# Transposed attention blocks kept in DRAM by the row that reads them, half of q and v loaded once, and a new time table

## The chip, the cores and the metric

The kernel runs on one core of one Trainium2 chip. The metric is the time of one execution on the device, in microseconds (us). Smaller is better.

A core has a matrix engine (TensorE, PE in the profile, with its weight loads as PEld), a vector engine (VectorE, DVE), a scalar engine (ScalarE, ACT), a general engine (GpSimd, POOL) and a synchronisation engine (SyncE, SP). Each works through its own list of instructions in the order in which the program wrote them, and waits on semaphores for what the others make. All of this kernel's DMAs are issued by SP. SP does not wait for a DMA to land, unless the next instruction in its list needs what the DMA brings, or needs a buffer that something still reads.

## The reference

Attention within chunks of 64 positions, with the softmax inside the chunk; then the heads are laid side by side and go through a layer that takes the largest of three products, and an output projection. All is float32.

```python
scores = scale * np.matmul(q_c, k_c.transpose(0, 1, 2, 4, 3))     # 8 x 8 heads x 9 chunks, 64 x 64
scores = scores - np.max(scores, axis=-1, keepdims=True)
attn = np.exp(scores)
attn = attn / (np.sum(attn, axis=-1, keepdims=True) + 1e-09)
x = np.matmul(attn, v_c)                                          # -> (4608, 512)
h = np.maximum(np.maximum(x @ w1, x @ w2), x @ w3)                # 512 -> 768
out = h @ w_out                                                   # 768 -> 512
```

## The kernel before, in words

**Tiles and groups.** The 4608 rows are 36 tiles of 128 rows, and four tiles make a group; there are nine groups. For one group TensorE makes 18 blocks of "hidden" products (6 columns blocks times three weights) and four output tiles. Each float32 matrix is held as two parts, a rounded high part and the rest, and a product is three matmuls (`three`, lines 168 to 171): 128x512 each. In the planner's account a triple of them is one step of 0.6815 us. The last two groups are taken together by another scheme (`pair`), in which TensorE alone sets the pace.

**The attention of a tile.** The first 8 tiles take a plain path at the start. The other 28 are made by `attention` (from line 270). For one of them the steps are, with the names that the time table uses:

- `r0`, `r1`: q and k are loaded into the two halves of the tile `r` (line 320), `rv`: v is loaded into `rv` (line 325). In DRAM each is kept twice, so that partitions 0 to 63 and 64 to 127 receive the same numbers.
- `qh`/`ql`, `vh`/`vl` (`stack`, lines 307 and 311): ACT rounds the tile into `qs` or `vs`, and then partitions 64 to 127 are overwritten with what the rounding left over, by DVE for q and by POOL for v. The high part thus stands in the upper 64 partitions and the low part in the lower 64, and one matmul over 128 partitions adds both.
- `kh`/`kl` (lines 333 and 337): high and low part of k, in two halves `c`, side by side in `kk`.
- `s0`, `s1` with `sa0`, `sa1` (`products`, lines 289, 295, 300): four matmuls each, whose two partial results ACT and DVE bring together in `e`.
- `mx`, `sub`, `exp`, `sum`, `nrm`: the softmax, on DVE, POOL, ACT, DVE, POOL.
- `T`, `ah`, `al` (lines 379, 384, 388): DVE transposes 32x32 blocks, and ACT and DVE make the high and the low part, in one tile `ah`.
- `there` (line 393): `ah` is written to DRAM. `aa` (line 400): it is read back, once to partitions 0 to 63 and once to 64 to 127, because each row of the matmul needs pieces from four groups of 32 partitions. That is two DMAs of 512 KB. The tile `aa` has one buffer.
- `x0`, `x1` with `xa0`, `xa1` (line 289, 295, 300): the products with v, four matmuls each, and `xh`, `xl`: high and low part of the result, which the hidden products of a later group read. For the last two groups the result goes to `stage` instead.

**What sets the order.** A planner written in the kernel walks along TensorE's own work, the triples of the groups, with a clock `now`. Every step of a tile has a time in a table, relative to that tile's `s0`, and is written into the program when `now` reaches it. So the table fixes the order on each engine; when a step really runs follows from that order and from the semaphores. The first four of the 28 tiles take the table `AT`, and one of them follows another after 18 us; the other 24 take `MOVED`, with 14.9 us from one to the next. So the work of three tiles is under way at a time: TensorE meets `s0` and `s1` of tile t+1 before `x0` of tile t, and `s1` of tile t+2 behind it.

**Other steps named below.** `spill` writes the sum of two weight parts to DRAM (line 508, `whole<-f`), `output` stores finished tiles (line 480, `out_x<-ao`); both go through SP. `OPERANDS`, `FIRST_MIXED`, `SP0` and `SP1` are due times of the preparation of the last two groups.

Of the kernel before, what the change touches and what calls it, by code (L numbers as in the profile page):

```python
# [20 lines left out]
P = 128  # L21
# [11 lines left out]
MOVED = {'r0': -18.9, 'r1': -14.6, 'rv': 7.3, 'qh': -8.4, 'ql': -7.2, 'kh0': -7.1, 'kl0': -6.2, 'kh1': -5.6, 'kl1': -1.4, 'sa0': 1.3, 's1': 3.3, 'sa1': 4.3, 'mx': 4.6, 'sub': 5.9, 'exp': 6.9, 'sum': 7.9, 'nrm': 9.1, 'T': 10.5, 'ah': 11.6, 'al': 11.7, 'there': 13.9, 'aa': 16.3, 'vh': 16.8, 'vl': 18.3, 'x0': 24.6, 'xa0': 25.6, 'x1': 28.3, 'xa1': 29.6, 'xh': 30.6, 'xl': 31.4}  # L33
EVERY = [18.3, 15.6]
OPERANDS = 5.4
FIRST_MIXED = 5.6
SECOND_MIXED = 5.6
SP0 = 10.4
SP1 = 12.0
TURN = [*range(12), 20, 21, *range(12, 16), 22, 23, *range(16, 20), *range(24, 28)]  # L40
ORDER = (1, 2, 5, 6, 7, 4, 3)
C0 = 17.3
C1 = 14.9
LEAD = 1.0
# [27 lines left out]
def chunk_attn_maxout_kernel(  # L72
# [196 lines left out]
    def attention(t, x_of, col, every, stage=None, moved=()):  # L269
# [32 lines left out]
        def stack(at, low_at, name, tag, src, eng):  # L302

            @due(at)
            def _():
                st[name] = att.tile([P, 2, 4, P], F32R, name=name, tag=tag, bufs=1)
                nc.scalar.copy(out=st[name], in_=src())  # L307

            @due(low_at)
            def _():  # L310
                eng.tensor_tensor(out=st[name][64:], in0=src()[64:], in1=st[name][64:].bitcast(F32), op=ALU.subtract)  # L311


        for half, at in enumerate((at_["r0"], at_["r1"])):
            @due(at)
            def _(half=half):
                if "r" not in loaded:
                    loaded["r"] = att.tile([P, 2, 2, 4, P], F32, name="r", tag="raw", bufs=1)
                st["r"] = loaded["r"]
                nc.sync.dma_start(out=st["r"][:, half], in_=qk2[t - PLAIN][:, half])  # L320

        @due(at_["rv"])
        def _():
            st["rv"] = att.tile([P, 2, 4, P], F32, name="rv", tag="rv", bufs=1)
            nc.sync.dma_start(out=st["rv"], in_=v2[t - PLAIN])
# [64 lines left out]
        @due(at_["there"])  # L390
        def _():
            st["there"] = dram.tile([4, 64, 512], F32, name="there")
            nc.sync.dma_start(out=st["there"].rearrange("n (l k) f -> (n l) k f", k=2),
                              in_=st["ah"].bitcast(F32).rearrange("p k a n x -> p k (a n x)"))

        @due(at_["aa"])
        def _():
            st["aa"] = att.tile([P, 4, 2, 8, 32], F32R, name="aa", tag="aa", bufs=1)
            for rows in halves_of:
                nc.sync.dma_start(out=st["aa"][rows].bitcast(F32).rearrange("p n a g x -> p n (a g x)"),  # L400
                                  in_=st["there"].rearrange("n p f -> p n f"))
# [520 lines left out]
```

## Time and profile before

| what | value |
|---|---|
| time, median of 3 runs | 716.36 us (711.51, 716.36, 722.11) |
| the profiled execution | 720.41 us on the device, span of its instructions 718.6 us |
| TensorE busy | 691.3 us, 96% of the span |
| VectorE, ScalarE, GpSimd busy | 516.7, 376.5, 249.9 us |
| DMA packets of the kernel's own queue | 125.32 MB, 57.8% of 16 engines' time |

The profile shows one execution. "Busy" of an engine counts its instructions, not its waits. A group of instructions is shown as its line, engine and operation, the tile that it writes and those that it reads, its count, its busy time and the mean of one, and the idle time of the engine just before it with what ended that. The chain of waits follows the work that ended last back from its end, at each step to what released it. A DMA is shown by its issue on SP ("SPq") and by the time from its issue to its landing. The granted clock of TensorE stands in the rows by stretch (PEclk; 1.00 is full speed).

### The profile page before, as it was taken

The page shows a single profiled execution, that of the slowest core. Times are in us where ns is not written, and L with a number is a line of the kernel's source. Part 1 is how long each engine was busy: PE and PEld are TensorE (multiplying, and loading weights), DVE is VectorE, ACT ScalarE, POOL GpSimd, SP SyncE. Part 2 cuts the span into 40 slices and gives each one's busy share as a digit, 9 for nine tenths or more (in the row PEclk, how much of TensorE's full clock was granted, in tenths as well). Part 3 has the DMA queues.
Part 4 walks back from the last instruction along what each step waited for, and adds up shares of the span by engine and source line. Part 5 has one row for each costly group of instructions (what it writes and reads, how often), then busy time and mean ns, then how long its engine had stood idle before and what let it go on. Part 6 is the DMA issues. An engine that isn't in the chain of part 4 may idle for free.

```text
span 718.6 us, 9620 instructions
## 1 busy us (share of the span) xinstructions
PE 691.3 (96%) x3336; PEld 574.5 (80%) x3336; DVE 516.7 (72%) x868; ACT 376.5 (52%) x695; POOL 249.9 (35%) x182
## 2 busy tenths in 40 slices
PE   8999999998899999999999998999989999999997
PEld 5998888887778777878877777878778888888876
DVE  6699984777668876898577876788657486768630
ACT  4476754554655566566656654566555352334221
POOL 1232201333334344222432332223323438666510
PEclk9599999999999999999999999999999999999999
DMA  8765554565787879667887767677784401011011
GB/s 344 304 226 180 205 176 138 173 207 172 224 258 215 220 209 277 177 202 213 236 232 194 214 175 236 195 212 193 194 257 123 131 30 59 29 31 26 5 55 63
DMA packets 44944, 125.93 MB, mean 175 GB/s; under 512 B 4192, under 2 KB 4192, under 8 KB 44896
## 3 DMA queue, kind: packets, MB, share of 16 engines
q1 hardware_dynamic: 44896, 125.32, 57.8%
q8 instruction: 26, 0.43, 0.3%
q14 instruction: 22, 0.18, 0.1%
HBM read 98.83 MB, written 26.48 MB: 174 GB/s over the span
## 4 chain that ended last, share of the span: by engine, by line
PE 29%; DMA 15%; DVE 13%; POOL 8%; ACT 4%; issue 3%; SPq 1%; POOLq 0%; ACTq 0%; DVEq 0%
DMA aa<-there 11%; PE pm L169 8%; PE pm L171 8%; PE pm L170 8%; DMA there<-ah 4%; PE x L289 3%; POOL c L537 2%; PE s L289 2%; POOL e L667 2%; DVE c L543 2%; POOL m L670 1%; DVE e L300 1%; POOL e L186 1%; POOL f L523 1%; ACT e L295 1%
## 5 line engine op out<-in xcount | busy, mean ns | idle before, releaser
L169 PE MATMUL pm<-xh,wl 128*128 128x512 f32 (+1 forms) x516 | 201.7, 391 | 0.0
L171 PE MATMUL pm<-xh,wh 128*128 128x512 f32 (+1 forms) x516 | 200.5, 389 | 0.0
L170 PE MATMUL pm<-xl,wh 128*128 128x512 f32 (+1 forms) x516 | 200.2, 388 | 0.0
L311 POOL TENSOR_TENSOR vs<-rv,vs 64x1024 fp32r<-64x1024 f32 x28 | 67.2, 2401 | 205.9 <-ACT vs L307 160.4
L171 PEld LDWEIGHTS pm<-xh,wh 128*128 128x128 f32 x516 | 98.0, 190 | 20.6
L169 PEld LDWEIGHTS pm<-xh,wl 128*128 128x128 f32 x516 | 98.3, 191 | 16.6
L170 PEld LDWEIGHTS pm<-xl,wh 128*128 128x128 f32 x516 | 98.1, 190 | 16.6
L300 DVE TENSOR_TENSOR e<-s,e 64x256 f32<-64x256 f32 x112 | 47.2, 422 | 47.6 <-ACT e L295 46.4
L458 DVE TENSOR_TENSOR m<-pm,m 128x512 f32<-128x512 f32 (+1 forms) x86 | 58.2, 677 | 11.9 <-PE pm L171 9.7
L169 PE MATMUL pm<-woh,h 128*128 128x512 f32 x168 | 65.6, 391 | 0.0
L170 PE MATMUL pm<-wol,h 128*128 128x512 f32 x168 | 65.6, 390 | 0.0
L171 PE MATMUL pm<-woh,h 128*128 128x512 f32 x168 | 65.5, 390 | 0.0
L186 POOL TENSOR_TENSOR e<-e,sm 128x512 f32<-128x512 f32 x30 | 37.6, 1253 | 73.4 <-DVE sm L183 58.4
L289 PEld LDWEIGHTS x<-aa,vs 128*128 128x128 f32 x224 | 32.4, 188 | 32.0 <-issue 17.5
L289 PE MATMUL x<-aa,vs 128*128 128x256 f32 x224 | 37.8, 291 | 20.0 <-DMA aa<-there 16.2
L295 ACT COPY e<-s 64x256 f32<-64x256 f32 x112 | 41.1, 367 | 28.5 <-PE s L289 27.5
L359 POOL TENSOR_TENSOR e<-e,mx 128x512 f32<-128x512 f32 x28 | 36.9, 1318 | 37.3 <-DVE mx L355 37.3
L464 ACT CAST h<-m 128x512 fp32r<-128x512 f32 (+1 forms) x43 | 26.2, 609 | 41.6 <-DVE m L458 41.4
L295 ACT COPY xs<-x 64x256 f32<-64x256 f32 x80 | 29.4, 368 | 33.2 <-PE x L289 32.5
L300 DVE TENSOR_TENSOR xs<-x,xs 64x256 f32<-64x256 f32 x80 | 33.4, 417 | 12.4 <-ACT xs L295 10.5
L337 DVE TENSOR_TENSOR kk<-r,kk 128x512 fp32r<-128x512 f32 x56 | 41.3, 739 | 1.0 <-ACT kk L333 0.8
L311 DVE TENSOR_TENSOR qs<-r,qs 64x1024 fp32r<-64x1024 f32 x28 | 37.5, 1340 | 6.1 <-ACT qs L307 5.4
(121 smaller groups left out, 1293.6 us busy)
## 6 DMA issues: line engine op xcount, KB each, us to landing
r<-in_qk SPq DMA_DIRECT2D x56, 512.0 KB, 4.6
aa<-there SPq DMA_DIRECT2D x56, 512.0 KB, 6.8
rv<-in_v SPq DMA_DIRECT2D x28, 512.0 KB, 5.5
there<-ah SPq DMA_DIRECT2D x28, 512.0 KB, 2.8
out_x<-ao SPq DMA_DIRECT2D x36, 256.0 KB, 2.1
buf<-in_qk SPq DMA_DIRECT2D x8, 768.0 KB, 7.2
buf<-in_w SPq DMA_DIRECT2D x10, 512.0 KB, 3.4
buf<-in_vb SPq DMA_DIRECT2D x8, 512.0 KB, 4.3
```

The source lines that it names most:

```text
L169: nc.tensor.matmul(out=o, lhsT=al, rhs=bh, start=first, stop=False)
L170: nc.tensor.matmul(out=o, lhsT=ah, rhs=bl, start=False, stop=False)
L171: nc.tensor.matmul(out=o, lhsT=ah, rhs=bh, start=False, stop=last)
L186: eng.tensor_tensor(out=e, in0=e, in1=sm.unsqueeze(2).broadcast_to([P, 8, 64]), op=ALU.mult)
L289: nc.tensor.matmul(out=o[:, g].rearrange("p a h x -> p (a h x)"), lhsT=lhs(g), rhs=rhs(g), start=True, stop=True)
L295: nc.scalar.copy(out=out()[rows], in_=st[name][rows, :, 0, h, :])
L300: nc.vector.tensor_tensor(out=out()[rows], in0=st[name][rows, :, 1, h, :], in1=out()[rows], op=ALU.add)
L311: eng.tensor_tensor(out=st[name][64:], in0=src()[64:], in1=st[name][64:].bitcast(F32), op=ALU.subtract)
L337: nc.vector.tensor_tensor(out=st["kk"][:, c, :, 1, :], in0=st["r"][:, 1, c], in1=st["kk"][:, c, :, 0, :].bitcast(F32), op=ALU.subtract)
L359: nc.gpsimd.tensor_tensor(out=e_all(), in0=e_all(), in1=st["mx"].unsqueeze(2).broadcast_to([P, 8, 64]), op=ALU.subtract)
L458: nc.vector.tensor_tensor(out=banks[j][:, :n], in0=ps[j, w][:, :n], in1=banks[j][:, :n], op=ALU.max)
L464: nc.scalar.copy(out=hh[j][:, lo:hi], in_=banks[j][:, :hi - lo])
```

## The change

Four things change.

- `there` is laid out as 64 rows of four pieces of 512 numbers, instead of four blocks of 64 rows. What one partition of `aa` reads, 8 KB, then lies in one piece. [...] The two reads stay two DMAs of 512 KB.
- q and v are loaded to partitions 0 to 63 alone: 256 KB instead of 512 KB each. `stack` rounds those 64 partitions, and makes the low part in partitions 64 to 127 from partitions 0 to 63. The k half of `r` is loaded to 128 partitions as before.
- The 24 tiles behind the first four have a new time table `MOVED`.
- Some planner constants change: where the first tile ends, the lead of the 24 tiles, and due times of the last two groups' preparation.

```diff
-MOVED = {'r0': -18.9, 'r1': -14.6, 'rv': 7.3, 'qh': -8.4, 'ql': -7.2, 'kh0': -7.1, 'kl0': -6.2, 'kh1': -5.6, 'kl1': -1.4, 'sa0': 1.3, 's1': 3.3, 'sa1': 4.3, 'mx': 4.6, 'sub': 5.9, 'exp': 6.9, 'sum': 7.9, 'nrm': 9.1, 'T': 10.5, 'ah': 11.6, 'al': 11.7, 'there': 13.9, 'aa': 16.3, 'vh': 16.8, 'vl': 18.3, 'x0': 24.6, 'xa0': 25.6, 'x1': 28.3, 'xa1': 29.6, 'xh': 30.6, 'xl': 31.4}
+MOVED = {'r0': -18.8, 'r1': -13.4, 'rv': 10.4, 'qh': -8.4, 'ql': -7.5, 'kh0': -7.7, 'kl0': -6.8, 'kh1': -4.5, 'kl1': 1.0, 'sa0': 2.5, 's1': 4.3, 'sa1': 5.5, 'mx': 5.9, 'sub': 7.6, 'exp': 7.9, 'sum': 9.2, 'nrm': 10.1, 'T': 12.1, 'ah': 12.6, 'al': 12.7, 'there': 13.2, 'aa': 17.0, 'vh': 19.3, 'vl': 20.1, 'x0': 26.1, 'xa0': 27.1, 'x1': 29.8, 'xa1': 31.6, 'xh': 32.6, 'xl': 33.4}
-OPERANDS = 5.4
-FIRST_MIXED = 5.6
+OPERANDS = 4.8
+FIRST_MIXED = 6.0
...
-SP1 = 12.0
+SP1 = 12.2
...
-C0 = 17.3
+C0 = 17.1
...
-LEAD = 1.0
+LEAD = 0.6
...
-                nc.scalar.copy(out=st[name], in_=src())
+                nc.scalar.copy(out=st[name][:64], in_=src()[:64])
...
-                eng.tensor_tensor(out=st[name][64:], in0=src()[64:], in1=st[name][64:].bitcast(F32), op=ALU.subtract)
+                eng.tensor_tensor(out=st[name][64:], in0=src()[:64], in1=st[name][:64].bitcast(F32), op=ALU.subtract)
...
-                nc.sync.dma_start(out=st["r"][:, half], in_=qk2[t - PLAIN][:, half])
+                rows = slice(0, P if half else 64)
+                nc.sync.dma_start(out=st["r"][rows, half], in_=qk2[t - PLAIN][rows, half])
...
-            nc.sync.dma_start(out=st["rv"], in_=v2[t - PLAIN])
+            nc.sync.dma_start(out=st["rv"][:64], in_=v2[t - PLAIN][:64])
...
-            st["there"] = dram.tile([4, 64, 512], F32, name="there")
-            nc.sync.dma_start(out=st["there"].rearrange("n (l k) f -> (n l) k f", k=2),
-                              in_=st["ah"].bitcast(F32).rearrange("p k a n x -> p k (a n x)"))
+            st["there"] = dram.tile([64, 4, 512], F32, name="there")
+            for n in range(4):
+                nc.sync.dma_start(out=st["there"][:, n].rearrange("(l k) f -> l k f", k=2),
+                                  in_=st["ah"][32 * n:32 * n + 32].bitcast(F32).rearrange("p k a g x -> p k (a g x)"))
...
-                nc.sync.dma_start(out=st["aa"][rows].bitcast(F32).rearrange("p n a g x -> p n (a g x)"),
-                                  in_=st["there"].rearrange("n p f -> p n f"))
+                nc.sync.dma_start(out=st["aa"][rows].bitcast(F32).rearrange("p n a g x -> p (n a g x)"),
+                                  in_=st["there"].rearrange("p n f -> p (n f)"))
```

What the new table does to the order is shown at three places, as rows of an engine's list; a row is the line, the operation, the tile written and the tiles read, the size, and how often it stands there. The changed kernel's lines are one or two higher than those of before.

TensorE, where the sixteenth of the 28 tiles' list is met. `x<-aa` is an `x1`, `s<-kk` the `s0` of the tile after the next; the rows between are a triple of the output projection. Before:

```order
L289 MATMUL x<-aa,vs 128x256 x4
L169 MATMUL pm<-woh,h 128x512
L170 MATMUL pm<-wol,h 128x512
L171 MATMUL pm<-woh,h 128x512
L289 MATMUL s<-kk,qs 128x256 x4
```

The same place now:

```order
L169 MATMUL pm<-woh,h 128x512
L170 MATMUL pm<-wol,h 128x512
L171 MATMUL pm<-woh,h 128x512
L289 MATMUL x<-aa,vs 128x256 x4
L289 MATMUL s<-kk,qs 128x256 x4
```

`s0` stays where it was and `x1` moved behind the triple. In the list of the 24 tiles `s1` stands one triple later than before and `x0` two triples later, so that between `s1` and `x0` of a tile there is one triple more than before in 20 tiles; in four tiles near the end the count is the same.

VectorE, the stretch from the maximum (`mx`) to the low part (`ah`) of the sixteenth tile. `qs` and `kk` belong to the next tile's q and k, `sm` is the sum, `m` the hidden products' maximum, `et` the transposition, `xs` the additions behind the tile before's `x0`. Before:

```order
L355 TENSOR_REDUCE mx<-e 128x8
L311 TENSOR_TENSOR qs<-r,qs 64x1024
L177 TENSOR_REDUCE sm<-e 128x8
L180 TENSOR_SCALAR sm<-sm 128x8
L183 RECIPROCAL sm<-sm 128x8
L337 TENSOR_TENSOR kk<-r,kk 128x4x128
L458 TENSOR_TENSOR m<-pm,m 128x512
L379 STREAM_TRANSPOSE et<-e 128x512
L300 TENSOR_TENSOR xs<-x,xs 64x4x64 x2
L388 TENSOR_TENSOR ah<-et,ah 128x2x256
```

Now:

```order
L356 TENSOR_REDUCE mx<-e 128x8
L311 TENSOR_TENSOR qs<-r,qs 64x1024
L338 TENSOR_TENSOR kk<-r,kk 128x4x128
L177 TENSOR_REDUCE sm<-e 128x8
L180 TENSOR_SCALAR sm<-sm 128x8
L183 RECIPROCAL sm<-sm 128x8
L460 TENSOR_TENSOR m<-pm,m 128x512
L380 STREAM_TRANSPOSE et<-e 128x512
L300 TENSOR_TENSOR xs<-x,xs 64x4x64 x2
L389 TENSOR_TENSOR ah<-et,ah 128x2x256
```

The low part of k (`kl0`) moved from behind the sum to ahead of it. The additions of the tile before still stand between the transposition and `ah`.

SyncE, one tile's DMAs in the middle of the run, where no output is stored. Before:

```order
L325 DMA rv<-in_v 128x1024
L320 DMA r<-in_qk 128x1024
L393 DMA there<-ah 128x1024
L320 DMA r<-in_qk 128x1024
L400 DMA aa<-there 64x4x512 x2
```

Now:

```order
L326 DMA rv<-in_v 64x1024
L321 DMA r<-in_qk 64x1024
L395 DMA there<-ah 64x1x512 x4
L321 DMA r<-in_qk 128x1024
L402 DMA aa<-there 64x2048 x2
```

The sequence is the same; one write became four, and three of the transfers have another shape.

## The prediction

> **What bounds the kernel now.** First the head of the page, then TensorE's busy time by stretch (columns: stretch, TensorE busy and its matmuls, weight loads, DVE, ACT, POOL, granted clock, DMA share, GB/s).
>
> ```profile
> PE 691.3 (96%) x3336; PEld 574.5 (80%) x3336; DVE 516.7 (72%) x868; ACT 376.5 (52%) x695; POOL 249.9 (35%) x182
> ```
> ```profile
> 200.00:600.00 400.00, 383.38 (x1820) 316.56 (x1819) 303.02 (x507) 226.93 (x425) 139.69 (x86) 0.99 0.70 198
> 600.00:690.00 90.00, 90.00 (x399) 74.39 (x398) 64.04 (x94) 29.85 (x53) 56.15 (x56) 1.00 0.08 21
> ```
>
> TensorE is the bound: without its idle time the span of 718.6 would be 691.3. From 600 us on it never waits; what can be won or lost lies before. The groups by line with their shapes kept apart name the place (behind the second bar: idle time just before, and what ended it):
>
> ```profile
> L289 PE MATMUL x<-aa,vs 128*128 128x256 f32 x224 | 37.8, 291 | 20.0 <-DMA aa<-there 16.2 <-issue 2.7 <-DVE stage L300 0.6
> L289 PE MATMUL s<-kk,qs 128*128 128x256 f32 x224 | 36.0, 283 | 1.3 <-DVE e L300 1.3
> ```
>
> 20.0 of the 27.3 us that TensorE idles stand ahead of `x0` and `x1`, and most of it are waits for `aa`. Their number and the longest stand in the table of waits (us in total, times, longest):
>
> ```profile
> PE x L289 <- DMA aa<-there: 16.2, 14, 2.5
> ```
>  The chain of waits shows what `aa` waits for (start, duration, what; one tile and the start of the next):
>
> ```profile
> 351.33 0.70 DVE ah L388
> 352.05 2.98 DMA there<-ah
> 355.08 0.58 SPq L400
> 355.71 8.77 DMA aa<-there
> ...
> 364.62 0.73 PE x L289 x4
> ...
> 366.58 0.43 DVE xs L300
> 367.04 0.70 DVE ah L388
> 367.76 2.81 DMA there<-ah
> ```
>
> `ah` is stored (2.98), read back (0.58 for the first issue, 8.77 for the second read), and only then does `x0` run: 12.6 us from the end of `ah`. The median DMAs (size, us to landing) and the range for `aa`:
>
> ```profile
> r<-in_qk SPq DMA_DIRECT2D x56, 512.0 KB, 4.6
> aa<-there SPq DMA_DIRECT2D x56, 512.0 KB, 6.8
> rv<-in_v SPq DMA_DIRECT2D x28, 512.0 KB, 5.5
> there<-ah SPq DMA_DIRECT2D x28, 512.0 KB, 2.8
> out_x<-ao SPq DMA_DIRECT2D x36, 256.0 KB, 2.1
> ```
> ```profile
> DMA to landing us min/median/max: 4.8/6.8/9.4
> ```
>
> **How a stall is passed on.** `s1` of tile t+1 stands before `x0` of tile t in TensorE's list, `s1` of tile t+2 behind it. If `x0` of t waits, tile t+1 gets that much more time for its softmax and its DMAs, tile t+2 does not. So a path that is too long by d makes two neighbours wait d together, d/2 on average: over 24 tiles, 1 us of path is worth 12 us. This holds while the path is longer than its room. Waits come irregularly (14 of 28 are put down to `aa`), so that a gain shrinks as more tiles stop waiting; 12 is an upper estimate for gains. There is a second loop: the additions behind `x0` of t stand on DVE ahead of `ah` of t+1. From `x0` at 364.62 to the end of that `ah` at 367.74 it is 3.1 us. With the median DMAs, 2.8 + 0.6 + 6.8 = 10.2, a round takes 13.3, less than the 14.9 of the table. With the slow ones of the chain, 12.6, it takes 15.7 and binds, which is why this pair stands on the chain. I take the first loop for the sum; the second starts to bind all over only if the DMAs rise by 1.6.
>
> **The change part by part.**
>
> *TensorE's order.* `x0` stands two triples later and `s1` one. A matmul takes 90.00/399 = 0.226, a triple 0.68: that much more room in 20 of 24 tiles, 0.57 on average. The work is the same and there is no other cost on TensorE; it was the idle time that was the cost. **-0.57 per tile.** One answer, from the order.
>
> *VectorE's order.* `kl0` stands ahead of the sum. Two tiles of the trace show what covers it (start, duration, engine, line, and idle time before it with its releaser):
>
> ```profile
> 331.15 0.69 DVE L467 TENSOR_TENSOR h<-m,h 128x512 fp32r<-128x512 f32 x1
> 331.76 0.68 DVE L177 TENSOR_REDUCE sm<-e 128x8 f32<-128x512 f32 x1
> 332.48 0.17 DVE L180 TENSOR_SCALAR sm<-sm 128x8 f32<-128x8 f32 x1
> 332.68 0.20 DVE L183 RECIPROCAL sm<-sm 128x8 f32<-128x8 f32 x1
> 332.80 0.65 DVE L337 TENSOR_TENSOR kk<-r,kk 128x512 fp32r<-128x512 f32 x1
> ```
> ```profile
> 347.05 0.69 DVE L177 TENSOR_REDUCE sm<-e 128x8 f32<-128x512 f32 x1 [1.60 <-ACT e L364]
> ```
>
> In the first tile DVE was the late one at the sum, and another 0.65 ahead of it would be paid in full. In the second the sum waited 1.60 for the exponential, and `kl0` would have fitted in. Bounds 0 to 0.65; I take the middle, **+0.35**. Its place behind the sum becomes free, but there DVE waits for POOL anyway, so I count no gain.
>
> *Halves of q and v.* The rounding on ACT and the subtraction take as many elements per partition as before. Reading from one half of the partitions and writing to the other is not in the trace; the nearest rows are the same subtractions within one half:
>
> ```profile
> L311 POOL TENSOR_TENSOR vs<-rv,vs 64x1024 fp32r<-64x1024 f32 x28 | 67.2, 2401 | 205.9 <-ACT vs L307 160.4
> L311 DVE TENSOR_TENSOR qs<-r,qs 64x1024 fp32r<-64x1024 f32 x28 | 37.5, 1340 | 6.1 <-ACT qs L307 5.4
> ```
>
> I take them unchanged: the same engines walk the same 1024 elements. POOL, busy 35% of the span, covers a moderate rise. Of the loads, the bytes halve, but do the DMA engines get free earlier? Three stretches in which one kind of transfer runs: `there` (128 partitions), the second `aa` read (64 partitions), `r` (128).
>
> ```profile
> 562.20:563.20 1.00, 1.00 (x8) 0.88 (x7) 0.24 (x1) 0.29 (x1) 0.00 (x0) 1.00 0.97 393
> 568.60:570.40 1.80, 1.80 (x9) 1.49 (x9) 0.00 (x0) 0.00 (x0) 1.29 (x2) 1.00 1.11 217
> 128.00:128.80 0.80, 0.80 (x7) 0.76 (x6) 0.80 (x2) 0.10 (x1) 0.00 (x0) 1.00 1.02 405
> ```
>
> All three keep the DMA engines fully busy, at 393 and 405 GB/s with 128 partitions and at 217 with 64. At that rate 256 KB to 64 partitions take 1.2 us, 512 KB to 128 take 1.3. So I give the halved loads nothing of their own; between 0 and the 0.65 us that half the bytes would save at the full rate, and that only where a load runs beside `aa`. It is part of the low end for `aa` below.
>
> [...]
>
> *Four writes for one.* The next write can be issued 0.33 us later at best (its issue's duration, below), or 0.6 like an `aa` issue.
>
> ```profile
> L400 SPq DMA_DIRECT2D aa<-there x56: 579/606/674, 120.5 to 564.7; - x56
> L393 SPq DMA_DIRECT2D there<-ah x28: 326/327/1337, 117.2 to 561.4; - x28
> ```
>
> The last write is issued 1.0 to 1.9 us behind the first. If it lands like the 256 KB of `out_x`, 2.1, all is there after 3.1 to 4.0 instead of 2.8; being half that size it might land some 0.5 sooner, so 2.6 is the low end. If 32 rows run at the rate of 64, the 512 KB take 2.4 us rather than 1.3, which also gives some 3.9. Bounds -0.2 to +1.2; the nearest row is `out_x` with the short issue, and with a part for the slower rate I take **+0.6**. Behind these issues on SP stand `r1` and `aa`; `aa` waits for the landing anyway. `r1` waits for `kl1`, which stands behind `ah` on DVE as before.
>
> *Reads of 8 KB.* A quarter of the pieces should shorten the 0.58 of an issue, and so the second read by some 0.3. The transfer keeps its rate if 217 GB/s is set by the 64 partitions: 1 MB then needs 4.8. The fastest landing seen is 4.8 against a median of 6.8, and `rv` is issued into it, as SP's list shows; with half of `rv` less is in the way.
>
> ```profile
> 370.63 1.24 SPq L400 DMA_DIRECT2D aa<-there  x2
> 375.63 0.33 SPq L325 DMA_DIRECT2D rv<-in_v  x1
> ```
>
> Bounds -1.6 (near the fastest) to +0.3 (nothing won, and `r1` closer ahead). Middle, **-0.7**.
>
> *The first four tiles* keep their table, but `C0` puts `x0` of two of them a triple earlier. That is up to 0.68 each; the DMA terms nearly cancel. **+0.5 in all** (-1 to +2).
>
> *The last two groups' preparation* is hidden: TensorE is busy 90.00 of 90.00 there.
>
> *The clock.* Two stretches show a lower one:
>
> ```profile
> 440.00:460.00 20.00, 17.71 (x79) 14.46 (x78) 12.80 (x23) 9.96 (x20) 4.76 (x3) 0.91 0.79 226
> 520.00:540.00 20.00, 17.82 (x79) 14.54 (x78) 11.57 (x22) 10.42 (x19) 5.59 (x5) 0.91 0.87 236
> ```
>
> 0.09 of 20 us is 1.8 us each. Both come some us after long waits for `aa`, the longest 2.5; that these cause them is my reading. With shorter waits I let one go, **-1.8** (0 to -3.6). [...] The rows have the lower clock, whatever made it.
>
> **The sum.** Per tile -0.57 + 0.35 + 0.6 - 0.7 = -0.32; times 12 = -3.8. With +0.5 and -1.8: -5.1. The profiled execution was 720.4 (span 718.6 and 1.8 around it), so 715.3. The median of three runs is 4.0 lower, probably from fewer long waits; the same step from there gives **711 us**.
>
> **The rivals.**
>
> *Slower: the writes land late and the reads win nothing.* `there` takes +1.2, and the reads stay as they are because the 64 partitions set their rate. Per tile -0.57 + 0.35 + 1.2 = +0.98, times 12 = +11.8; the first four tiles pay 1.2 each less what is idle, +3: 716.4 + 15 = 731. For it: one rate for all 64-row transfers, and 32 rows can hardly do better. Against it: reads of 6.8 are far above the 4.8 that the rate allows. It is slower from +1.2 us per tile on; below that within 2%. Chance 0.17. [...]
>
> *Faster: the reads reach their rate.* `aa` at 5.3 instead of 6.8: -0.57 + 0.35 + 0.6 - 1.5 = -1.1, times 12 = -13; of 20.0 us some 4 to 7 remain. Both clock dips go, -3.6: about 699. For it: the low rate of `aa` has a cause other than the 64 partitions, since the second read lands 8.77 after its issue in the chain. Against: the trace shows no 8 KB piece. Chance 0.25.
>
> *No change: room won by the table goes to SP's list.* `aa` stands behind `r1`, and `r1` behind `kl1` on DVE. If that comes 0.3 later than the landing of `there`, the sum is zero: 716. Chance 0.18. The forecast keeps 0.40.
>
> About 2% is what a measurement here can tell from no change, 14 us. Faster by more has the second rival's 0.25; slower the first one's 0.17; the rest 0.58. The range: the second rival's 699 with 1 us more, and on the other side two thirds of the way to the first, 698 to 727.
>
> **What would show it.** `x<-aa,vs` idle time falls from 20.0 to about 16, and the waits of `aa` with it. `there` lands 3.2 to 3.6 after the first issue, `aa` in 6 to 6.5. DMA share between 200 and 600 stays near 0.70 although bytes fall. The subtractions keep 1340 and 2401 ns. It is wrong if `there` reaches 4, if `x0` waits for something other than `aa`, or if TensorE's waits move to `s`.

## The result, and the profile after

| | before | after |
|---|---|---|
| time, median | 713.93 us (711.36 to 722.11, 4 runs) | 735.29 us (734.57 to 746.32, 4 runs) |
| profiled execution: time, span | 720.41, 718.6 us | 734.57, 732.8 us |
| TensorE busy | 691.3 us | 689.1 us |
| idle ahead of `x` / ahead of `s` | 20.0 / 1.3 us | 36.2 / 1.1 us |
| bytes of the kernel's own DMA queue | 125.32 MB | 110.65 MB |

The ratio is 1.0308, with a 95% interval of 1.0241 to 1.0375; it leaves out one slow run of each kernel (722.11 and 746.32 us). The change made the kernel slower by 3%, some 21 us, although it moves 12% fewer bytes.

The head of the changed kernel's page:

```profile
PE 689.1 (94%) x3336; PEld 570.4 (78%) x3336; DVE 514.1 (70%) x868; ACT 377.3 (51%) x695; POOL 255.2 (35%) x182
```

TensorE is busy equally long within 2.2 us, so what separates these two executions is idle time. (Their granted clocks, 0.983 and 0.985, are nearly equal too, but for different reasons; the part on the clock below comes back to it.) The groups by line with the shapes kept apart say where it lies (behind the second bar: idle time just before, and what ended it):

```profile
L289 PE MATMUL x<-aa,vs 128*128 128x256 f32 x224 | 38.4, 294 | 36.2 <-DMA aa<-there 29.0 <-issue 3.8 <-POOL e L186 2.6
L289 PE MATMUL s<-kk,qs 128*128 128x256 f32 x224 | 36.2, 284 | 1.1 <-DVE e L300 0.9
```

The table of waits gives the number and the longest (us in total, times, longest):

```profile
PE x L289 <- DMA aa<-there: 29.0, 18, 3.2
```

It is the same place as before, `x0` waiting for `aa`, with 16.2 us more. That is more than the whole growth of the span, 14.2; the clock and the rest gave 2.0 back. The chain of waits shows one such wait (start, duration, what):

```profile
341.02 0.43 DVE stage L300
...
341.48 0.70 DVE ah L389
342.20 0.59 SPq L395
...
342.83 0.60 SPq L395
...
343.47 0.60 SPq L395
...
344.12 2.36 DMA there<-ah
...
346.61 0.47 SPq L402
...
347.14 7.31 DMA aa<-there
...
354.58 0.72 PE x L289 x4
```

Where one write of 2.98 us stood, there are now three issues of 0.6 us in a row and then a fourth write of 2.36. The additions of the tile before (`stage`, line 300) stand on the chain directly ahead of `ah`, as `xs` did at 366.58 in the chain of before. The DMA issues (size, median us from issue to landing):

```profile
aa<-there SPq DMA_DIRECT2D x56, 512.0 KB, 7.2
r<-in_qk SPq DMA_DIRECT2D x28, 512.0 KB, 4.6
there<-ah SPq DMA_DIRECT2D x112, 128.0 KB, 2.4
...
r<-in_qk SPq DMA_DIRECT2D x28, 256.0 KB, 5.6
rv<-in_v SPq DMA_DIRECT2D x28, 256.0 KB, 6.1
```

A write of 128 KB lands after 2.4 us, nearly as late as the one of 512 KB did (2.8). The reads of `aa` went from 6.8 to 7.2, and the halved loads land later than the full ones did (`rv` 6.1 after 5.5). How long SP takes to issue them (minimum, median, maximum in ns) stands in the view of the tile `there`:

```profile
L395 SPq DMA_DIRECT2D there<-ah x112: 549/596/1279, 108.7 to 577.2; - x112
L402 SPq DMA_DIRECT2D aa<-there x56: 470/538/1224, 113.2 to 580.3; - x56
```

The windows (columns as in the prediction: TensorE, weight loads, DVE, ACT, POOL, granted clock, DMA share, GB/s) show the main stretch, then a moment in which only these writes run, one in which only `aa` reads of 8 KB pieces run, and the five stretches of 20 us with a low clock:

```profile
200.00:600.00 400.00, 369.36 (x1735) 303.45 (x1734) 284.91 (x497) 218.89 (x413) 130.88 (x79) 0.98 0.67 164
344.00:345.00 1.00, 1.00 (x6) 0.80 (x5) 0.51 (x2) 0.96 (x4) 0.00 (x0) 1.00 0.86 203
349.20:351.80 2.60, 2.60 (x13) 2.17 (x12) 2.53 (x3) 0.68 (x2) 1.76 (x1) 1.00 1.00 246
180.00:200.00 20.00, 18.95 (x84) 15.80 (x85) 10.01 (x19) 11.58 (x22) 6.71 (x4) 0.91 0.72 188
280.00:300.00 20.00, 16.81 (x70) 13.77 (x69) 12.15 (x21) 8.85 (x18) 4.97 (x4) 0.83 0.69 171
360.00:380.00 20.00, 17.51 (x78) 14.32 (x77) 11.76 (x23) 9.45 (x19) 5.44 (x3) 0.91 0.76 184
420.00:440.00 20.00, 18.04 (x83) 14.72 (x82) 13.41 (x25) 10.67 (x20) 6.36 (x4) 0.91 0.57 138
460.00:480.00 20.00, 17.81 (x83) 14.74 (x82) 13.25 (x24) 10.13 (x20) 4.50 (x3) 0.91 0.65 147
```

In that moment the writes from 32 partitions kept the DMA engines busy for 0.86 of the time and moved 203 GB/s. The one write from 128 partitions moved 393 (before, 562.2 to 563.2).

For the steps of a tile I followed each of the tiles 6 to 28 through the trace, from the end of its `s1` to the landing of its second read; these are medians, in us:

| | before | after |
|---|---|---|
| end of `s1` to end of `ah` (softmax, transposition) | 10.68 | 10.96 |
| first write's issue to the last landing | 2.81 | 4.34 |
| first read's issue to the last landing | 8.20 | 8.50 |
| the whole way | 22.18 | 24.34 |
| start of `x0` of the tile before to end of `ah` | 4.01 | 3.12 |

The whole way grew by 2.16 us, and 1.53 of it is the writes. At the 0.57 us more room that the table gives, 1.6 us a tile is left over. By the prediction's rule that 1 us of path is worth 12 us of time, that makes 19; the idle time ahead of `x` grew by 16.2.

### The profile page after: what moved, and what is told of

It is laid out like the page before. It is cut to its first block, busy times and chain, and to the rows that moved or that the text cites. A ratio compares the mean times of both kernels' runs of the same rounds, so it can differ in the third digit from the quotient of the medians.

```text
span 732.8 us, 9756 instructions
## 1 busy us (share of the span) xinstructions
PE 689.1 (94%) x3336; PEld 570.4 (78%) x3336; DVE 514.1 (70%) x868; ACT 377.3 (51%) x695; POOL 255.2 (35%) x182
## 3 DMA queue, kind: packets, MB, share of 16 engines
q1 hardware_dynamic: 35488, 110.65, 55.6%
## 4 chain that ended last, share of the span: by engine, by line
PE 40%; DMA 24%; DVE 14%; POOL 8%; ACT 5%; issue 4%; SPq 3%; POOLq 0%; DVEq 0%; ACTq 0%
DMA aa<-there 14%; PE pm L169 10%; PE pm L170 10%; PE pm L171 10%; DMA there<-ah 3%; DMA r<-in_qk 3%; PE x L289 3%; PE s L289 2%; SPq L395 2%; PE x L252 2%; POOL c L539 2%; DVE e L300 2%; POOL e L669 2%; DVE c L545 1%; PE s L209 1%
## 5 line engine op out<-in xcount | busy, mean ns | idle before, releaser
L311 POOL TENSOR_TENSOR vs<-rv,vs 64x1024 fp32r<-64x1024 f32 x28 | 68.3, 2441 | 228.4 <-ACT vs L307 205.1
L289 PE MATMUL x<-aa,vs 128*128 128x256 f32 x224 | 38.4, 294 | 36.2 <-DMA aa<-there 29.0
L186 POOL TENSOR_TENSOR e<-e,sm 128x512 f32<-128x512 f32 x30 | 32.7, 1092 | 78.4 <-DVE sm L183 71.3
L360 POOL TENSOR_TENSOR e<-e,mx 128x512 f32<-128x512 f32 x28 | 45.6, 1630 | 26.0 <-DVE mx L356 25.1
L338 DVE TENSOR_TENSOR kk<-r,kk 128x512 fp32r<-128x512 f32 x56 | 45.4, 813 | 11.9 <-ACT kk L334 11.4
L334 ACT CAST kk<-r 128x512 fp32r<-128x512 f32 x56 | 34.2, 617 | 17.3 <-DMA r<-in_qk 17.0
```

The source lines that it names most:

```text
L186: eng.tensor_tensor(out=e, in0=e, in1=sm.unsqueeze(2).broadcast_to([P, 8, 64]), op=ALU.mult)
L289: nc.tensor.matmul(out=o[:, g].rearrange("p a h x -> p (a h x)"), lhsT=lhs(g), rhs=rhs(g), start=True, stop=True)
L311: eng.tensor_tensor(out=st[name][64:], in0=src()[:64], in1=st[name][:64].bitcast(F32), op=ALU.subtract)
L334: nc.scalar.copy(out=st["kk"][:, c, :, 0, :], in_=st["r"][:, 1, c])
L338: nc.vector.tensor_tensor(out=st["kk"][:, c, :, 1, :], in0=st["r"][:, 1, c], in1=st["kk"][:, c, :, 0, :].bitcast(F32), op=ALU.subtract)
L360: nc.gpsimd.tensor_tensor(out=e_all(), in0=e_all(), in1=st["mx"].unsqueeze(2).broadcast_to([P, 8, 64]), op=ALU.subtract)
```

## The experiments

Three parts can be taken apart: the table, the halves of q and v, and the layout (four writes and 8 KB reads). Kernels were timed on different chips, so the ratios to the kernel before are compared, which was run beside each.

### The table alone

The kernel before with the new `MOVED` and the new constants.

```diff
-MOVED = {'r0': -18.9, ...
+MOVED = {'r0': -18.8, ...
-C0 = 17.3
+C0 = 17.1
```

> The kernel before with the new time table and planner constants alone; transfers as before. Theory W (the four writes land 1.6 us later, 4.4 instead of 2.8, and that is the loss): the table by itself gives x0 0.6 us more room and costs the softmax path 0.3 to 0.5, so 708 to 718, ratio 0.99 to 1.005, idle time before the x products 16 to 20 us. Theory T (the new order on VectorE and SyncE, kl0 ahead of the sum and r1 close ahead of aa, is the loss): over 725, ratio over 1.015, idle over 28.

Measured: 714.42 us, ratio 0.9932 (0.9880 to 0.9984). Idle ahead of `x` is 19.2. The table is worth 0.7%, about 5 us. The prediction had -0.22 us a tile for it, -2.6 in all, which the interval contains. The table isn't the cause of the loss. The way from the end of `s1` to `ah` is 10.58 us here, no longer than the 10.68 of before; the part on why the prediction was wrong comes back to this.

### The halves of q and v alone

```diff
-                nc.sync.dma_start(out=st["r"][:, half], in_=qk2[t - PLAIN][:, half])
+                rows = slice(0, P if half else 64)
+                nc.sync.dma_start(out=st["r"][rows, half], in_=qk2[t - PLAIN][rows, half])
...
-            nc.sync.dma_start(out=st["rv"], in_=v2[t - PLAIN])
+            nc.sync.dma_start(out=st["rv"][:64], in_=v2[t - PLAIN][:64])
```

> The kernel before with q and v loaded to half the partitions alone; old table, old writes and reads. Theory W: no difference, 711 to 718, ratio 0.995 to 1.005; the 256 KB loads land within 0.5 us of the 512 KB ones (4.6 and 5.5). [...]

Measured: 707.91 us, ratio 0.9866 (0.9807 to 0.9924). The wait and the DMA issues of this kernel:

```profile
PE x L289 <- DMA aa<-there: 8.0, 9, 1.9
```
```profile
aa<-there SPq DMA_DIRECT2D x56, 512.0 KB, 6.6
...
r<-in_qk SPq DMA_DIRECT2D x28, 256.0 KB, 3.5
rv<-in_v SPq DMA_DIRECT2D x28, 256.0 KB, 5.1
```

The halves are worth 1.3%, where I had counted nothing. The waits for `aa` fell from 16.2 to 8.0, and `aa` lands in 6.6 instead of 6.8. The way from `s1` to the second landing became 0.33 us shorter (21.85 after 22.18), which by the rule of 12 makes 4 us; the idle time ahead of `x` fell by as much (15.8 after 20.0). The ratio says 5.5 to 14 us. A part of what lies above 4 goes with the clock: three of the four runs have a granted clock of 0.995 to 0.998, the runs of before beside them 0.987 to 0.994. At the same clock, 0.988, it is 714.42 us against 719.62 to 720.64, some 5 to 6 us. Why the clock is higher with the halves, no run tested.

### The layout alone

```diff
-            st["there"] = dram.tile([4, 64, 512], F32, name="there")
-            nc.sync.dma_start(out=st["there"].rearrange("n (l k) f -> (n l) k f", k=2),
+            st["there"] = dram.tile([64, 4, 512], F32, name="there")
+            for n in range(4):
+                nc.sync.dma_start(out=st["there"][:, n].rearrange("(l k) f -> l k f", k=2),
```

> The kernel before with the new DRAM layout alone: four writes of 32 rows, reads of 8 KB pieces, old table. Theory W: the whole loss and more, since the old table leaves 0.6 us less room: there lands after 4.3, 735 to 748, ratio 1.03 to 1.05, idle before the x products 36 to 48. [...]

Measured: 751.01 us, ratio 1.0445 (1.0387 to 1.0503). The groups:

```profile
L289 PE MATMUL x<-aa,vs 128*128 128x256 f32 x224 | 39.2, 299 | 46.0 <-DMA aa<-there 40.9 <-POOL e L186 2.9 <-POOL e L359 1.5
```

The layout alone costs 4.4%, some 32 us, and the idle time ahead of `x` grows by 26.0. Here the whole loss of the change is found, and more. The table and the halves win part of it back.

### The changed kernel with the old layout

```diff
-            st["there"] = dram.tile([64, 4, 512], F32, name="there")
-            for n in range(4):
+            st["there"] = dram.tile([4, 64, 512], F32, name="there")
+            nc.sync.dma_start(out=st["there"].rearrange("n (l k) f -> (n l) k f", k=2),
```

> The changed kernel with the old layout put back: one write of 128 rows and reads of 2 KB pieces, with the new table and the halved loads. Theory W: the loss is gone, 706 to 716, ratio 0.985 to 1.003, there at 2.6 to 2.8. [...]

Measured: 708.54 us, ratio 0.9848 (0.9785 to 0.9910). The groups:

```profile
L289 PE MATMUL x<-aa,vs 128*128 128x256 f32 x224 | 37.5, 290 | 11.8 <-DMA aa<-there 9.7 <-DVE xs L300 1.0 <-POOL e L186 0.9
```

Without the layout the change is 1.5% faster than before. It is not measurably better than the halves alone (0.9866). Against the changed kernel the ratio is 4.6% lower, some 33 us: this is what the layout costs inside the change. Between the two traced executions it is 29.3 us of span; the idle time ahead of `x` is 24.4 lower, and TensorE is busy 7.2 us less, at a granted clock of 0.997 against 0.985.

### One write, 8 KB reads

The layout has two halves, writes and reads. Here one write of 128 rows takes the place of the four, and the reads keep their 8 KB pieces. The blocks then lie in another order in DRAM than the readers expect, so that the result is not the reference's; the sizes are those of the change.

```diff
-            for n in range(4):
-                nc.sync.dma_start(out=st["there"][:, n].rearrange("(l k) f -> l k f", k=2), ...
+            nc.sync.dma_start(out=st["there"].rearrange("p n f -> (p n f)").rearrange("(q e) -> q e", q=P), ...
```

> The changed kernel with one write of 128 rows instead of four, straight through the DRAM tile, so that the blocks lie in another order than the readers expect (the attention output is then not the reference's; all else is done as before); the two reads of 8 KB pieces stay. It prices the reads alone. Theory W (only the writes lose): there lands at 2.6 to 2.8, 702 to 714, ratio 0.98 to 1.0, near the kernel with table and halves but the old layout (0.985). Theory R (the 8 KB reads are slower than the 2 KB ones as well): aa 0.3 or more above 6.9, and the ratio at 1.0 to 1.015.

Measured: 704.76 us, ratio 0.9852 (0.9796 to 0.9909), the same as with the old layout. The DMA issues:

```profile
aa<-there SPq DMA_DIRECT2D x56, 512.0 KB, 7.2
...
there<-ah SPq DMA_DIRECT2D x28, 512.0 KB, 2.7
```

Pieces of 8 KB make the reads no faster: 7.2, where pieces of 2 KB had 6.8 before and 6.9 in the kernel of the last experiment. Nor was their rate higher in stretches in which only the two reads were under way, first two of before (2 KB), then three of the changed kernel (8 KB):

```profile
294.20:296.90 2.70, 2.70 (x15) 2.28 (x14) 1.47 (x3) 2.00 (x4) 2.36 (x1) 1.00 1.07 250
454.20:456.70 2.50, 2.50 (x14) 2.15 (x13) 0.58 (x3) 1.92 (x4) 2.38 (x1) 1.00 1.06 230
```
```profile
264.10:267.70 3.60, 3.60 (x17) 2.98 (x16) 3.50 (x4) 1.40 (x3) 2.54 (x2) 1.00 0.99 234
382.10:384.30 2.20, 2.20 (x12) 1.79 (x11) 1.28 (x3) 2.07 (x4) 2.17 (x1) 1.00 1.00 246
433.20:437.40 4.20, 4.20 (x20) 3.46 (x19) 3.69 (x5) 1.98 (x4) 3.98 (x2) 1.00 0.87 193
```

In the time they cost nothing measurable, within the 0.6% of the intervals. On the path they may: from the first read's issue to the last landing it is 8.96 us, against 8.43 with the old layout, and the idle time ahead of `x` is 14.8 against 11.8. So the four writes carry the loss; what the reads may add is small, some 3 us of idle time here.

### Four writes into the old layout

The changed kernel with the old layout and 2 KB reads, but still four writes of 32 rows. A row now writes one piece of 4 KB; in the change it writes two of 2 KB.

```diff
-            st["there"] = dram.tile([64, 4, 512], F32, name="there")
+            st["there"] = dram.tile([4, 64, 512], F32, name="there")
...
-                nc.sync.dma_start(out=st["there"][:, n].rearrange("(l k) f -> l k f", k=2),
+                nc.sync.dma_start(out=st["there"][n].rearrange("(l k) f -> l k f", k=2),
```

> The changed kernel with the old layout, but written by four DMAs of 32 rows (4 KB pieces); reads of 2 KB pieces as before. It prices the four writes alone. Theory W: there 4.0 to 4.5, 728 to 742, ratio 1.02 to 1.035, as the changed kernel. Theory L (the 2 KB pieces scattered at 8 KB distance are what is slow, not the number of writes or their rows): there under 3.3 and a ratio under 1.0.

Measured: 719.58 us, ratio 1.0032 (0.9989 to 1.0075). The groups, the view of the tile `there`, and a moment with only these writes:

```profile
L289 PE MATMUL x<-aa,vs 128*128 128x256 f32 x224 | 38.5, 295 | 21.6 <-DMA aa<-there 16.2 <-issue 2.7 <-POOL e L186 1.6
```
```profile
L395 SPq DMA_DIRECT2D there<-ah x112: 302/421/1307, 117.7 to 566.0; - x112
```
```profile
339.60:340.40 0.80, 0.80 (x5) 0.64 (x4) 0.80 (x2) 0.77 (x3) 0.00 (x0) 1.00 1.03 236
```

The time lies between those of the two theories, and two prices come apart. Dividing the write into four costs 1.8% (0.9848 to 1.0032), and cutting each row into two pieces 2.8% more (to 1.0308). The 8 KB reads come with the second step; by the experiment before they cost little, but that kernel had more slack, so a part of the 2.8% may be theirs. In this kernel an issue takes 0.42 us and all is landed 3.52 us after the first issue, against 2.67 for the single write; in the change an issue takes 0.60 and the landing 4.34. In both the writes run at about half the rate of the single one, 236 and 203 GB/s against 393.

### The four writes issued by two engines

If it is the issues of 0.6 us in a row, two engines that issue should help. Here ScalarE issues every second write.

```diff
-                nc.sync.dma_start(out=st["there"][:, n].rearrange("(l k) f -> l k f", k=2),
+                (nc.sync, nc.scalar)[n % 2].dma_start(out=st["there"][:, n].rearrange("(l k) f -> l k f", k=2),
```

> The changed kernel with the second and fourth write issued by ScalarE, whose queue then takes half of the issues. Theory I (four issues of 0.6 us one after another on SyncE make the delay): the last write is issued 0.6 instead of 1.9 us behind the first and all have landed at 3.0 to 3.2; 712 to 722. Theory P (32 rows reach the DMA engines at half rate, and the four transfers take 4 x 0.6 us one after another however they are issued): 3.6 to 4.0; 722 to 732. ScalarE pays 2 x 0.6 us per tile for the issues in either case.

Measured: 735.75 us, ratio 1.0294 (1.0224 to 1.0365), no different from the change. The landing of all four took 3.99 instead of 4.34; each write lands later:

```profile
there<-ah ACTq DMA_DIRECT2D x56, 128.0 KB, 2.9
there<-ah SPq DMA_DIRECT2D x56, 128.0 KB, 3.2
```

The last write now goes out 0.63 us behind the first instead of 1.92. With the issues side by side each write landed 0.5 to 0.8 us later than the 2.4 of the change, and only 0.35 us is won. The idle time ahead of `x` fell to 26.5, but 8.2 now stand ahead of `s`, which waits 7.9 for DVE. An issue takes 0.607 us on ScalarE (median), and a tile has two. That these delay the way that brings `s` out is my reading; the gain is paid there.

### The two reads issued by two engines

A miss. I had thought that the two reads, one into each half of the partitions, could together run at the 393 to 405 GB/s of transfers with 128 partitions if they started together. This is the kernel before, its second read issued by ScalarE.

```diff
-            for rows in halves_of:
-                nc.sync.dma_start(out=st["aa"][rows].bitcast(F32).rearrange("p n a g x -> p n (a g x)"),
+            for rows, queue in zip(halves_of, (nc.sync, nc.scalar)):
+                queue.dma_start(out=st["aa"][rows].bitcast(F32).rearrange("p n a g x -> p n (a g x)"),
```

> The kernel before with the second read of aa issued by ScalarE instead of SyncE, old table, old layout. [...] If the transfers go one after another all the same: 8 us and 712 to 722, with some loss for ScalarE, which waits for the landing of there.

Measured: 731.71 us, ratio 1.0184 (1.0074 to 1.0294). The DMA issues:

```profile
aa<-there ACTq DMA_DIRECT2D x28, 512.0 KB, 8.1
aa<-there SPq DMA_DIRECT2D x28, 512.0 KB, 7.7
```

The second read now goes out 0.07 us behind the first, where it was 0.63. Both land about 8 us after their issue, and from the first issue to the last landing it is 8.39, against 8.20 with one engine. The traced execution is the longest of the four (736.33 us), so the 0.19 says little; but the gain that the idea needs is not there, by my estimate 1.6 to 1.9 us (1 MB takes 4.2 to 4.6 us at the 230 to 250 GB/s of the reads before, and 2.6 at 400). The time got worse, and the waits show one price: ScalarE now waits for `there` to land before it may issue. Whether that is all of it, the run doesn't show.

```profile
ACT vs L307 <- DMA there<-ah: 9.5, 5, 2.7
```

### More room, another order, both

The path is too long by about 1.6 us a tile. Does it help to give it room? Three kernels change the table of the changed kernel alone. One moves `x0` and all behind it one triple later:

```diff
-... 'x0': 26.1, 'xa0': 27.1, 'x1': 29.8, 'xa1': 31.6, 'xh': 32.6, 'xl': 33.4}
+... 'x0': 26.8, 'xa0': 27.5, 'x1': 30.5, 'xa1': 32.3, 'xh': 33.3, 'xl': 34.1}
```

> The changed kernel with x0 and what follows it due 0.7 us later, so that TensorE's list has one triple (0.68 us) more between s1 of a tile and its x0; the order on VectorE stays, the additions of a tile ahead of ah of the next one. In the changed kernel the way from the end of s1 to the landing of the second read is 24.3 us a tile and has room for 21.9, and the second loop (x0, additions, ah of the next tile, the four writes, the reads) takes 3.1 + 4.4 + 8.6 + 0.14 = 16.3 against the 14.9 of the table. Theory F (the first way alone binds): the wait shrinks by 0.34 a tile, some 8 us over 24 tiles: about 727 (722 to 730), idle time ahead of x 26 to 30 instead of 36. Theory L (the second loop binds, and room doesn't help it): no difference from the changed kernel, 732 to 738, idle time ahead of x 34 to 38. Both at once: between them, 729 to 733.

One leaves `x0` and moves its additions behind `ah` of the next tile:

```diff
-... 'x0': 26.1, 'xa0': 27.1, 'x1': 29.8, 'xa1': 31.6, 'xh': 32.6, 'xl': 33.4}
+... 'x0': 26.1, 'xa0': 28.7, 'x1': 31.9, 'xa1': 33.7, 'xh': 34.7, 'xl': 35.5}
-            @due(at + 0.6)
+            @due(at + (2.0 if name == 'x' and pool == 'ps_x' and at == MOVED['x0'] else 0.6))
```

> The changed kernel with x0 at its old time, but the copy of x0's result 1.4 us later and xa0, x1 and what follows 1.6 to 2.1 us later: ah and al of a tile now stand on VectorE ahead of the additions of the tile before, which opens the second loop; the room of the first way stays at 21.9. Theory L (the second loop binds): the end of al comes some 0.65 us earlier in most tiles: idle time ahead of x falls by 8 to 16 us, 720 to 728. Theory F (the first way alone binds): little difference, 731 to 738.

And one does both, with two triples:

```diff
-... 'x0': 26.1, 'xa0': 27.1, 'x1': 29.8, 'xa1': 31.6, 'xh': 32.6, 'xl': 33.4}
+... 'x0': 27.5, 'xa0': 28.7, 'x1': 31.2, 'xa1': 33.0, 'xh': 34.0, 'xl': 34.8}
```

> The changed kernel with two triples more room ahead of x0 (1.36 us) and with ah ahead of the additions of the tile before. If the two loops together carry the loss: the excess of the first way falls from 2.4 to about 1.0, which is 0.5 a tile and 12 us over 24 tiles, less the idle time that stays: 713 to 722, idle time ahead of x 16 to 24. If the loss lies elsewhere (more half-clock windows, queues, DMAs in each other's way): above 728.

Room alone: 734.93 us, ratio 1.0292 (1.0208 to 1.0376), no difference. The groups:

```profile
L289 PE MATMUL x<-aa,vs 128*128 128x256 f32 x224 | 38.4, 294 | 31.7 <-DMA aa<-there 24.8 <-POOL f L506 2.2 <-POOL e L186 1.7
L289 PE MATMUL s<-kk,qs 128*128 128x256 f32 x224 | 37.4, 290 | 5.2 <-DVE e L300 5.2
```

The wait of `x` fell by 4.5, half of the 8 that theory F gave, and `s` waits 4.1 more.

Order alone: 739.46 us, ratio 1.0335 (1.0246 to 1.0424), no difference from the change. The additions did get behind `ah`, but what follows them slid as well. DVE's timeline (start, duration, engine, line, operation):

```profile
401.32 0.86 DVE L300 TENSOR_TENSOR e<-s,e 64x256 f32<-64x256 f32 x2 [1.43 <-ACT e L295]
402.21 0.88 DVE L426 TENSOR_TENSOR xl<-xs,xh 128x512 fp32r<-128x512 f32 x1
403.01 0.67 DVE L356 TENSOR_REDUCE mx<-e 128x8 f32<-128x512 f32 x1
```

`xl` of an earlier tile now stands between the additions of `s1` and the maximum `mx`, with 0.88 us. From the end of `s1` to that of `mx` it takes 3.67 us (median over the tiles) instead of 2.40, and to that of `ah` 11.54 instead of 10.96: what was won ahead of `ah` was lost ahead of `mx`. So this run does not test the second loop cleanly, and theory L is neither shown nor refuted by it.

Both: 717.57 us, ratio 1.0066 (1.0025 to 1.0106). The waits:

```profile
PE x L289 <- DMA aa<-there: 10.0, 9, 3.0
PE x L289 <- DVE xs L300: 7.2, 9, 1.5
```

Here 2.4 of the 4.6% that the layout costs come back, some 17 us, with the writes as they were (4.29 to the last landing). The waits for `aa` fell by 19.0. The idle time ahead of `x` fell by only 10.9, to 25.3, since 7.2 now wait for DVE; the rest of the gain in the traced execution is other idle time and 4.9 us less of TensorE's busy time, at a granted clock of 0.995 instead of 0.985. That shows that about half of the loss is these waits for `aa` and what comes with them, and that room and order take it away together. Which of the two ways binds is not settled, since each of the single edits moved a wait to another place.

### The same table without the layout

The kernel with the new table, the halves and the old layout, now with the table of the last one.

> The kernel with the new table and the halved q and v but the old layout and its single write (708.5), with two triples more room ahead of x0 and ah ahead of the additions of the tile before. Idle time ahead of x was 11.8 there. If it is still the room that these waits lack (theory F): 2 to 6 us left, 698 to 704. If they come from single slow transfers that no room of 1.4 us covers: 705 to 710.

Measured: 708.98 us, ratio 0.9953 (0.9901 to 1.0004). The waits:

```profile
PE x L289 <- DVE xs L300: 9.9, 12, 1.6
PE x L289 <- DMA aa<-there: 5.1, 3, 2.2
```

The waits for `aa` fell from 9.7 to 5.1, but in their place `x` waits 9.9 for DVE's additions behind an earlier `x`. Where the path is short enough, the room costs what it brings: no gain over 0.9848. Of the kernels with the whole of the computation, the fastest are the halves alone and the table with the halves, at 0.987 and 0.985.

## Why the prediction was wrong

I had forecast 711 us within 698 to 727. It is 735.29; the change is slower by more than 2%, to which I had given 0.17. Point by point:

**TensorE's order and VectorE's order: the total near, the +0.35 not.** -0.57 + 0.35 a tile was put at -2.6 us; the table alone measures -0.7%, some 5 us. Its idle time ahead of `x` fell by only 0.8, so most of the 5 us did not come from there. And the +0.35 for `kl0` was not paid. With the table alone the way from `s1` to `ah` is 10.58 us after 10.68. DVE's groups for the sum, before and with the table alone, show where `kl0` went:

```profile
L177 DVE TENSOR_REDUCE sm<-e 128x8 f32<-128x512 f32 x36 | 24.6, 684 | 15.6 <-ACT e L364 13.8 <-ACT e L232 1.3
L177 DVE TENSOR_REDUCE sm<-e 128x8 f32<-128x512 f32 x36 | 24.5, 681 | 5.8 <-ACT e L364 4.6
```

The sum waited 13.8 us for the exponential and now waits 4.6: `kl0` went mostly into that wait, as in the second of the two tiles that the prediction showed. POOL's subtraction of the maximum takes 1630 ns on average in the changed kernel, which has this table too, instead of 1318. In the changed kernel the way from `s1` to `ah` did grow by 0.28, near the 0.35, but by luck: it comes with the layout. The layout alone, with the old table, has 11.07, and the new table with the old layout and the halves has 10.52. What may link the two is taken up under the second loop.

**Halves of q and v, wrong.** "I give the halved loads nothing of their own" rested on the time of one such load, 1.2 us instead of 1.3. Alone they bring 1.3%, some 4 us of it by a shorter path. That `qs` and `vs` take the old time was right:

```profile
L311 POOL TENSOR_TENSOR vs<-rv,vs 64x1024 fp32r<-64x1024 f32 x28 | 68.3, 2441 | 228.4 <-ACT vs L307 205.1 <-issue 23.3
```

2441 ns after 2401, and 1302 after 1340 on DVE.

**Four writes for one: here the forecast failed.** The term was +0.6 with bounds of -0.2 and +1.2; measured +1.53, beyond the upper bound. Two parts of it were too small. I took 0.33 us for an issue, the row of the 128-row write; the four take 0.596 each, and the last write goes out 1.92 us behind the first (342.20 to 344.12). And I let the last one land 2.1 us after its issue like `out_x`, or sooner since it is half the size; it is 2.4, and the writes from 32 partitions moved at about half the rate. The sentence that 32 rows may run at the rate of 64 stood in the prediction with 3.9 us as its result, and I gave it only a part. It is right: 203 GB/s in the change and 236 in the four writes of 4 KB pieces, against 393 from 128 partitions.

**Reads of 8 KB, wrong.** -0.7 was the middle between the fastest landing and nothing; measured +0.30, and +0.4 on the median landing (7.2 after 6.8). How much of that is the pieces' own is open: the kernel with the new table, the halves and the old layout has 8.43, the changed one 8.50, the one with 8 KB reads behind one write 8.96. The pieces got four times larger and the rate did not rise: 193 to 246 GB/s where pieces of 2 KB had 230 to 250. The 217 of the prediction is not the reads' alone: `ao<-whole`, 256 KB, was issued at 565.39 and landed 7.4 us later, so it too was under way in that stretch. The issue became shorter, 0.538 after 0.606 us, and nobody gained by it. With one write and 8 KB reads the time is that of the old layout within the intervals.

**The sum.** With the measured sizes it is -0.57 + 0.28 + 1.53 + 0.30 = +1.54 a tile, times 12 = +18. Idle time ahead of `x` grew by 16.2. With the layout alone the whole way is 24.83 us, 2.65 longer than before and without more room; the idle time grew by 26.0. Both make about 10 us of idle time for 1 us of path. So the way in which a stall is passed on held, and the factor of 12 nearly; the two DMA terms were mis-sized, +1.83 instead of -0.1 us a tile. The +0.5 for the first four tiles no run separates.

**The second loop.** I left it out unless the DMAs rose by 1.6. They rose by 1.83, and a round now takes 3.1 + 4.3 + 0.1 + 8.5 = 16.0 us against 14.9. In 12 of the 23 tiles looked at `ah` follows `x0` of the tile before at the shortest distance (3.2 us or less), in 6 before. It stands on the chain above. `ah` then waits for an `x0` that is itself late, which fits the 0.28 by which the way to `ah` grew. How much of the loss is its own, the runs didn't separate.

**The clock.** I let one stretch of low clock go, for shorter waits; the waits got longer and there are five stretches, four of 0.09 and one of 0.17 of 20 us: 1.8 and 3.4 us, 10.6 in all. In the profiled execution of before I had overlooked the largest loss, at its start (the windows of before):

```profile
0.00:20.00 20.00, 17.92 (x94) 12.54 (x95) 13.73 (x26) 9.23 (x14) 3.33 (x9) 0.90 0.91 352
20.00:40.00 20.00, 20.00 (x124) 20.00 (x124) 12.98 (x24) 10.83 (x21) 6.38 (x6) 0.67 0.80 306
```

0.10 and 0.33 of 20 us make 8.6 us. Executions of before with a granted clock of 0.992 and 0.995 have spans of 714.3 and 713.7. So the step of 4.0 down to the median, which I put down to fewer long waits, is more likely this start, and the two profiles differ by less (14.2) than the medians (21.4).

The changed kernel's traced execution has no such start. Behind it, the low clock takes 3.6 us of before and 10.6 of the changed kernel: +7.0 where I had -1.8. This is a second term that the prediction had wrong, and in its sign; by this estimate it is up to a third of the 21 us between the medians. It goes with the waits: with the same transfers and waits for `aa` of 10.0 us ("both"), eight of ten runs have a granted clock of 0.995 or more, the changed kernel's four 0.975 to 0.991. That the waits cause it is not shown.

**The rivals.** The first one came out as it says: "the writes land late and the reads win nothing", 731 us with +1.2 for `there`. With +1.53, the reads a little worse and the lower clock it became 735. What I held against it, reads far above the 4.8 that 217 GB/s give, was no evidence about writes. The second rival, reads at their rate, falls with the 8 KB reads behind one write: `aa` stayed at 7.2. The third, room lost in SP's list, isn't what happened: the reads follow the last landing after 0.14 us (median), and `r1` is issued while the writes are still under way (at 344.81 in the stretch above, where the last write lands at 346.48).

**What would show it.** The prediction named `there` at 4 as a sign that it is wrong; it is 4.34. That `x0` would go on waiting for `aa` and that the DMA share stays near 0.70 (0.67) held.

## What to carry to other kernels

Before a DMA is divided, count per part the issue on the queue and the partitions it touches: here four writes of 32 partitions cost four issues of 0.596 us one behind the other and moved 203 GB/s where the single one had moved 393, and on a path with no slack each microsecond came back about tenfold over 24 tiles. Larger pieces in DRAM won nothing here: reads into 64 partitions moved 193 to 246 GB/s in pieces of 8 KB and 230 to 250 in pieces of 2 KB. When the trace doesn't show an operation, and a row of a neighbouring shape (64 partitions at 217 GB/s) speaks for the worse end of the bounds, do not take the middle.

## What the runs showed of the hardware

- SP's issue of a write took 0.327 us (median, before) for 128 rows of one 4 KB piece each, 0.421 (the four writes into the old layout) for 32 such rows, and 0.596 (the change) for 32 rows of two 2 KB pieces. So it did not go with the size: 512, 128 and 128 KB.
- Writes from 32 partitions moved 203 GB/s (the change) and 236 (the four writes into the old layout). Reads into 64 partitions moved 230 to 250 (before) and 193 to 246 (the change), and transfers from or into 128 partitions 393 to 405 (before). Two reads into the two halves at once, from two engines, were no faster than one behind the other (8.39 and 8.20 us for both, medians of one execution each).
- In the changed kernel, whose longest wait for `aa` is 3.2 us, TensorE's granted clock fell to 0.50 five times, for 1.8 to 3.4 us of lost time each. Four of the five times it fell 0.7 to 1.4 us after a wait of 2.0 to 3.1 us for `aa` had ended, and once within a wait of 3.2; after another of 2.6, which ended at 254.3, it did not fall. What decides, no run tested.
